# Moving the first gate's score steps into PSUM, and handing over from attention to the experts in another order

## The chip, the cores and the metric

One core of a Trainium2 chip runs the whole program. The metric is the device time of one execution in microseconds (us); lower is better. The engines are named as in the profile: PE multiplies matrices (PEld is its weight load), DVE, ACT and POOL are the vector, scalar and GpSimd engines, SP issues most transfers. [...]

## What is computed

Three layers in a row, for 2 batches of 768 tokens, 512 wide:

```
mask   = q_cluster == k_cluster            # nearest of 16 centroids per head
attn   = softmax(where(mask, q k^T / 8, -1e9)) @ v      # 8 heads of 64
x      = concat of the heads                            # 1536 x 512
noisy  = x @ w_gate + log1p(exp(x @ w_noise)) * noise   # 8 experts
top 2 of noisy, weights by softmax over the two
out    = sum over the two of  weight * relu(x @ w1[e]) @ w2[e]
y      = soft mixture (32 slots, 8 experts) of out
```

The gate (scores, top 2, the place of each token in its expert's list) is computed with small vector operations on tiles of 48 or 24 numbers a partition.

## The kernel before, in words

**Attention.** The 16 (batch, head) pairs are worked two at a time: `NP` = 8 double heads p, of 12 steps each (2 halves of the queries, `qh`, by 6 blocks of keys, `kc`). A global step number s runs from 0 to 95; the main loop of `body` takes two steps at a time (`s0`). In one turn of the loop PE gets two units of row maxima for the next double head (`munit`, tiles `pmx` and `mp`), the two steps' scores (`score`, tile `psc`), and the products with the values of the two steps before (`av`, tile `pav`). ACT takes the exponential (`pt`, five buffers). `add` sums the `pt` tiles for the denominators: POOL the first blocks (`psa`), DVE the last ones (`psb`). After each half, `ot_evac` copies the product, `den` sums the partial sums with PE (`pden`, `dt`, `rd`), and `xout` multiplies with an identity and the gate weights (`px`) and writes rows of `x` and the gate products `gp`. Tables `pre`, `mid` and `post` say at which step each such call is issued; each engine works in the order of issue.

**Gates.** `gate` returns a list of small operations and a list of scatters. Gate 0 handles chunks 0 to 5 (batch 0, finished with double head 3), gate 1 chunks 6 to 8 and gate 2 chunks 9 to 11 (the two query halves of batch 1). They stand in one list `todo`, and `gap(s, n)` issues up to n entries of it at given places of the loop; an integer in the list ends a gap. Gate 0's operations are issued from step 56 on, nearly all on DVE with operands in SBUF, at a rate from the table `RATE`; its 12 scatters (`scatter`, an indirect transfer on POOL that writes 128 rows of `x` to the lists `xg` in memory) follow with `GN` = 3 empty entries ahead of each. Gates 1 and 2 come from step 96 on and within the first steps of the expert layer.

**Expert layer (`MoE1`).** Ten lists: experts 0 and 1 of batch 0 ("short lists", jobs 0 and 1 of 256 rows), the six others for all tokens, and the short lists of batch 1. Each job has 8 steps f. A step's weights are loaded (`load_w`, four buffers `WR`), split into a high part by ACT (`split_hi`, L833) and a low part by DVE, for some steps half by POOL (`split_lo`, L840, L842), and used by `first` (L935, 12 products, then `H` by ACT and DVE) and `second` (L976, 6 products for a short list). Six splits are made in the last double head (`SP`), the others three steps ahead. `load_x` loads a list's rows on SP; `prep_t`, `prep_h`, `prep_l` transpose them on DVE and split them (L890, L897, L903). For jobs 0 and 1 the load is issued at step 80, the preparation at steps 84 to 90.

**The hand-over.** `first(0)` is issued between the scores and the last `av` of step 96. The last half's `den` and `xout` are issued in the expert layer's steps 0 and 1 (`late`), with the gate operations of batch 1 between them. `rank` of gate 1 starts with five products of the identity that nobody reads (L613).

Of the kernel before, what the change touches and what calls it, by code (L numbers as in the profile page):

```python
# [6 lines left out]
F32 = mybir.dt.float32  # L7
# [43 lines left out]
X9 = 57  # L51
DL = 64
PH, PL = 1, 1
JT, JN, JH, JL = (0, 2), 2, 2, 3
SP = 1, 3, 5, 7, 8, 9
SL, MX = 1, 96
LT = 6, 8, 9
B1 = 9
B7 = 8
B2 = 1  # L60
TF = (0, 0), (0, 1)
RATE = 2, 1, 1, 1, 2, 3, 1, 2, 1, 1, 4, 1, 3
ORD, U1, Z1, R1, Z0 = (1, 1, 1, 0, 1, 0, 1, 1), 3, 8, 4, 2
M2S = 14, 15, 16, 18, 20
MS = 10, 10, 12, 14, 18
G0, GN, KS = 55, 3, 64


class Ctx:
# [15 lines left out]
class Attention:  # L85
# [294 lines left out]
    def av(self, p, t):  # L380
        nc, g = self.nc, self.g
        qh, kc = divmod(t, 6)
        pt = self.ptile[p, t]
        if kc == 0:
            self.avp[p, qh] = g.psum.tile([128, 512], F32, tag="av", name="pav")
        for hh in range(2):
            nc.tensor.matmul(self.avp[p, qh][64 * hh:64 * hh + 64, :384], self.vt[p][:, hh, kc, :],  # L387
                             pt[:, hh, :], start=(kc == 0), stop=(kc == 5))

    def add(self, p, t):  # L390

        qh, kc = divmod(t, 6)
        pt = self.ptile
        n = 6 if p == 0 else 4 if p < MASKED else 3
        first = 0 if kc < n else n
        if kc == first:
            return
        eng = self.nc.vector if first else self.nc.gpsimd
        if kc == first + 1:
            k = "b" if first else "a"  # L400
            s = (self.g.at if first else self.g.xp).tile([128, 2, 384], F32, name=f"ps{k}", tag=f"ps{k}",
                                                         bufs=1 if first else 2)
            self.stile[p, qh, k] = s
# [15 lines left out]

    def bank(self, p, qh, name):  # L420
        g = self.g
        if p == NP - 1 and qh == 0:
            return g.psum.tile([128, 512], F32, tag="mx", name=name, bufs=2)
        return g.pm.tile([128, 512], F32, tag="misc", name=name)

    def den(self, p, qh):
        nc, g = self.nc, self.g

        parts = [self.stile.pop((p, qh, k)) for k in "ab" if (p, qh, k) in self.stile]
        terms = [(hh, s.rearrange("p h (c a j) -> p h a c j", c=3, a=4)) for s in parts for hh in range(2)]  # L430
        ps = self.bank(p, qh, "pden")
        for i, (hh, s) in enumerate(terms):
            for a in range(4):
                nc.tensor.matmul(ps[32 * a:32 * a + 32, :96], self.sel[:, hh, :], s[:, hh, a, :],
                                 start=(i == 0), stop=(i == len(terms) - 1))
# [26 lines left out]
class Dispatch:  # L462
# [67 lines left out]

    NFILL = (NSL // 128 + 1) // 2 + (NTOK + NTRASH) // 256

    def gate(self, q, first, n):

        nc, g, xp = self.nc, self.g, self.g.xp
# [5 lines left out]
        place = g.place if q == 0 else g.again  # L541

        def t(name, *shape, dt=F32):
            if name not in T and q != 1:
                m = 1
                for x in shape:
                    m *= x
                names = " ".join("abc"[:len(shape)])
                a = place(m) if dt is F32 else place(m // 2).bitcast(dt)
# [56 lines left out]
        out.append(3 if b == 0 else 1)  # L606

        def rank():
            ps = g.pm.tile([128, 512], F32, tag="misc", name="prank")
            mb = MB()  # L610

            for i in range(5 if q == 1 else 0):
                nc.tensor.matmul(ps[:, 384:], g.ident, g.ident, start=True, stop=True)  # L613
            fl = lambda a: a.rearrange("p c e -> p (c e)")
            nc.tensor.matmul(ps[:, :n * E], self.tri, fl(mb), start=True, stop=False)
            for i in range(1, n):
# [13 lines left out]
        if b == 0:  # L630
            op(dv.memset, c1[:, 0:NREG], 0.0)
# [144 lines left out]
class MoE1:  # L776
# [58 lines left out]
    def split_lo(self, s):  # L835
        nc = self.nc
        hi, lo = self.ring[s]
        wr = self.wr.pop(s)
        n = 512 if self.short[self.steps[s][0]] and not 6 <= s < 13 and s < DL else 1024
        nc.vector.tensor_tensor(lo[:, :n], wr[:, :n], f32(hi)[:, :n], op=OP.subtract)  # L840
        if n < 1024:
            nc.gpsimd.tensor_tensor(lo[:, n:], wr[:, n:], f32(hi)[:, n:], op=OP.subtract)  # L842
# [501 lines left out]
def body(tc, qk, q2, k2, v2, cent, wgn, noise, w12, phi, v12, out):  # L1344
    nc = tc.nc
    with ExitStack() as ctx:
# [93 lines left out]
        for p in range(-1, NP):  # L1440
# [24 lines left out]
            if p >= 0:  # L1465
                for qh in range(2):
                    at(post, s0 + 6 * qh + 6, A.ot_evac, p, qh)
                    for s, fn in zip(LT if p == NP - 1 else (8, 10, 12), (A.total, A.den, A.xout)):
# [28 lines left out]
        a, z = gates[1][0], [f for f in gates[2][0] if type(f) is not int]  # L1497
        i = next(i for i, f in enumerate(a) if type(f) is int and i > 10) - 13
        a, x = a[:i], [f for f in a[i:] if type(f) is not int]
        y, z = z[:21], z[21:]  # L1500
        mix(MX, a, [], 1)
        turns = y[:2] + x[:3] + y[2:6] + x[3:6]
        x, y = x[6:], y[6:]
        while x or y:
            turns += x[:1] + y[:1]
            x, y = x[1:], y[1:]
        mix(99, turns, [], 1)
        k = next(i for i, f in enumerate(z) if f.__name__ == "rank")
        mix(99, z[:k] + [1] + z[k:], gates[1][1], 3)
        mix(99, [], gates[2][1], 1)  # L1510
        half = len(todo) - half
        quota = {1: (8, 16), 2: (14, 14), 3: (14, 14)}
# [23 lines left out]
        def load_x(j):  # L1536
            assert len(todo) <= half, (len(todo), half)
            M1.load_x(j)

        for j in range(2):  # L1540
            at(post, s0 - 4, load_x, j)
            s = s0 + JT[j]
            for i in range(JN):
                at(post, s + i, M1.prep_t, j, i, JN)
                at(post, s + i + JH, M1.prep_h, j, i, JN)
                at(post, s + i + JL, M1.prep_l, j, nc.vector if i % 2 else nc.gpsimd, i, JN)
        end = 12 * NP + 2
        for s0 in range(0, end, 2):
            k = RATE[s0 // 2 - 28] if 56 <= s0 < 82 else 1 if s0 < KS else 3 if s0 < 12 * NP else 0
            units = pre.get(s0, []) + pre.get(s0 + 1, [])  # L1550
            for s in (s0, s0 + 1):
                if units:
# [5 lines left out]
            for fn, a in units + mid.get(s0, []):  # L1558
                fn(*a)
            gap(s0, k)  # L1560
            if s0 == 12 * NP:
                M1.first(0)
            for s in (s0 - 2, s0 - 1):
                if 0 <= s < 12 * NP:
                    A.av(*divmod(s, 12))
                    A.add(*divmod(s, 12))
            for s in (s0, s0 + 1):
                for fn, a in post.get(s, ()):
                    fn(*a)
                gap(s0, k)  # L1570
        late = [x for s in sorted(post) if s >= end for x in post[s]]
        c_at.close()
        c_m2 = ctx.enter_context(ExitStack())
        M1.mo = enter(c_m2, "mo2")
# [3 lines left out]
        prep = {}  # L1578
        for j in range(2):
            at(prep, 5 + j, M1.prep_m, j)  # L1580
        for j in range(2, len(M1.jobs)):
            s, n, eng = PREP[j if j in PREP else 4]
            if j > 2:
# [6 lines left out]
        for s in range(ns):  # L1590
# [10 lines left out]
            if s + 1 < ns:  # L1601
                M1.first(s + 1)
            if s < NREG * NF:
                gap(1000 if s else 98, quota.get(s, (8, 8))[0])
# [6 lines left out]
            if s < 2:  # L1611
                fn, a = late[s]
                fn(*a)
            if s < NREG * NF:
                gap(1000 if s else 98, quota.get(s, (8, 8))[1])
# [107 lines left out]
```

## Time and profile before

| | |
|---|---|
| median of 3 runs | 652.12 us (650.39 to 652.66) |
| profiled execution | 650.09 us, span 648.30 us |
| mean granted TensorE clock | 0.981 |
| PE busy | 614.9 us, 95% |
| DVE busy | 409.0 us, 63% |
| ACT busy | 311.3 us, 48% |
| POOL busy | 289.3 us, 45% |

The times of the rows below are counted from the start of the span. Attention ends at about 250 us, the expert layer at about 585 us. [...] A bracket behind a row of a timeline tells how long the engine was idle ahead of it, and which event ended that.

### The profile page before, as it was taken

The numbers are of one execution on the slowest core, as the hardware profiler recorded it, in microseconds if no ns is written. First come the engines' busy times: TensorE is split into PE (matmuls) and PEld (weight loads), VectorE is DVE, ScalarE is ACT, GpSimd is POOL, SyncE is SP. The second block draws the span as 40 slices with busy tenths as digits, with TensorE's granted clock in tenths as the row PEclk, the third lists the DMA queues.
The fourth block names the chain that finished last, engine by engine and source line by source line (L and its number), as shares of the span: only waits on it lengthen the run. The fifth ranks groups of instructions, "written<-read, shape, count | busy, mean of one in ns | idle before, by whom it ended". The sixth has DMA issues, their size and how long they took to land. (4 is left out here: it accounts for less than half of the span.)

```text
span 648.3 us, 11039 instructions
## 1 busy us (share of the span) xinstructions
PE 614.9 (95%) x3967; PEld 472.8 (73%) x3967; DVE 409.0 (63%) x871; ACT 311.3 (48%) x444; POOL 289.3 (45%) x256
## 2 busy tenths in 40 slices
PE   7899999999799999789999999999999999998996
PEld 5567666676566657667888888888888888875544
DVE  6667888778965798566554445554544557645632
ACT  5576585765556582245334334443534445533002
POOL 3899676866758793543124033251423403110100
PEclk8699999999899999989999999999999999999999
DMA  8392845727255713478944829879796868978995
GB/s 317 76 267 79 287 149 179 252 89 275 95 191 167 209 66 131 156 223 232 196 133 110 218 98 272 298 255 258 278 281 234 167 207 276 321 269 271 425 398 198
DMA packets 62890, 139.47 MB, mean 215 GB/s; under 512 B 15280, under 2 KB 30832, under 8 KB 60784
## 3 DMA queue, kind: packets, MB, share of 16 engines
q1 hardware_dynamic: 56944, 125.31, 58.3%
q0 software_dynamic: 5888, 13.42, 9.5%
q8 instruction: 32, 0.52, 0.3%
q14 instruction: 26, 0.21, 0.1%
HBM read 108.18 MB, written 28.42 MB: 211 GB/s over the span
## 5 line engine op out<-in xcount | busy, mean ns | idle before, releaser
L976 PE MATMUL py<-ring,H 128*128 128x512 f32 (+1 forms) x686 | 172.9, 396 | 5.3 <-issue 3.5
L840 DVE TENSOR_TENSOR ring<-wr,ring 128x1024 fp32r<-128x1024 f32 (+1 forms) x77 | 93.5, 1214 | 100.4 <-ACT ring L833 99.5
L976 PEld LDWEIGHTS py<-ring,H 128*128 128x128 f32 (+1 forms) x686 | 123.9, 184 | 32.5 <-issue 3.8
L833 ACT ACTIVATE ring<-wr 128x1024 fp32r<-128x1024 f32 x77 | 81.5, 1059 | 91.7 <-PE py L976 83.6
L377 ACT ACTIVATE pt<-psc 128x768 f32<-128x768 f32 x96 | 77.2, 811 | 71.1 <-PE psc L374 60.8
L984 POOL DMA_INDIRECT x2acc<-y,mdi x31 | 50.2, 1621 | 104.4 <-ACT y L1009 97.6
L387 PE MATMUL pav<-pt,vt 128*64 128x384 f32 x384 | 73.6, 505 | 0.0
L941 ACT ACTIVATE H<-ph 128x256 fp32r<-128x256 f32 (+7 forms) x80 | 36.7, 459 | 75.9 <-PE ph L935 60.9
L338 DVE TENSOR_REDUCE mp<-pmx 128x1 f32<-128x512 f32 x96 | 63.2, 676 | 15.3 <-PE pmx L333 14.4
L935 PE MATMUL ph<-XS1a,ring 128*128 128x240 f32 (+3 forms) x288 | 67.8, 325 | 0.0
L407 POOL TENSOR_TENSOR psa<-psa,pt 128x768 f32<-128x768 f32 x32 | 61.9, 1936 | 4.7 <-ACT pt L377 2.5
L935 PE MATMUL ph<-XS0a,ring 128*128 128x432 f32 (+3 forms) x252 | 63.2, 332 | 0.1
L944 DVE SCALAR_TENSOR_TENSOR H<-ph,H 128x384 fp32r<-128x384 f32 (+2 forms) x120 | 43.4, 389 | 26.3 <-ACT H L941 20.6
L935 PEld LDWEIGHTS ph<-XS1a,ring 128*128 128x128 f32 x288 | 47.7, 188 | 3.6 <-DVE ring L840 0.2
L935 PE MATMUL ph<-XS0b,ring 128*128 128x256 f32 (+3 forms) x192 | 48.2, 325 | 0.8 <-DVE ring L840 0.6
L935 PE MATMUL ph<-XS1b,ring 128*128 128x240 f32 (+3 forms) x192 | 46.1, 313 | 0.8 <-DVE ring L840 0.8
L935 PEld LDWEIGHTS ph<-XS0a,ring 128*128 128x128 f32 x252 | 43.2, 188 | 4.0 <-issue 1.2
L903 POOL TENSOR_TENSOR XS0b<-xr,XS0a 128x512 fp32r<-128x512 f32 (+1 forms) x9 | 17.1, 1901 | 64.5 <-ACT XS0a L897 64.5
L387 PEld LDWEIGHTS pav<-pt,vt 128*64 128x64 f32 x384 | 23.5, 137 | 24.8 <-issue 19.3
L333 PE MATMUL pmx<-even 96*128 96x512 f32 (+1 forms) x96 | 34.0, 415 | 6.2 <-DVE mp L338 4.3
L343 DVE TENSOR_REDUCE mp<-pmx 128x2 f32<-128x512 f32 x48 | 33.0, 689 | 5.5 <-PE pmx L333 5.0
L638 POOL DMA_INDIRECT xg<-x,idx x24 | 25.9, 1077 | 21.1 <-DVE xr L567 14.8
(338 smaller groups left out, 1023.7 us busy)
## 6 DMA issues: line engine op xcount, KB each, us to landing
wr<-in_w SPq DMA_DIRECT2D x80, 512.0 KB
v<-in_v SPq DMA_DIRECT2D x9, 2048.0 KB
xg<-xr SPq DMA_DIRECT2D x14, 512.0 KB
wr<-in_qk SPq DMA_DIRECT2D x8, 768.0 KB
early<-in_q SPq DMA_DIRECT2D x8, 768.0 KB
early<-in_k SPq DMA_DIRECT2D x8, 768.0 KB
x2acc<-xr SPq DMA_DIRECT2D x8, 512.0 KB
vt<-in_v SPq DMA_DIRECT2D x8, 384.0 KB
```

Source lines behind the costliest of these rows:

```text
L333: nc.tensor.matmul(o, self.BQ[i][:96, qh, hh, 128 * c:128 * c + 128], self.BK[i][:96, hh, ks], start=True, stop=True)
L338: nc.vector.tensor_reduce(mp[:, 0, col:col + 1], ps, axis=AX.X, op=OP.max)
L377: nc.scalar.activation(pt, ps[:, :, :384], AF.Exp, scale=SCALE)
L387: nc.tensor.matmul(self.avp[p, qh][64 * hh:64 * hh + 64, :384], self.vt[p][:, hh, kc, :], pt[:, hh, :], start=(kc == 0), stop=(kc == 5))
L407: eng.tensor_tensor(s, s, pt.pop((p, t)), op=OP.add)
L833: self.nc.scalar.activation(self.ring[s][0], self.wr[s], AF.Copy)
L840: nc.vector.tensor_tensor(lo[:, :n], wr[:, :n], f32(hi)[:, :n], op=OP.subtract)
L935: nc.tensor.matmul(ph[:, :u], a[:, 128 * c:128 * c + 128], x[:, c, :u], start=(c == 0 and i == 0), stop=(c == 3 and i == 2))
L941: nc.scalar.activation(HH[:, :u], ph[:, :u], AF.Relu)
L944: nc.vector.scalar_tensor_tensor(o[:, :b - a], ph[:, a:b], 0.0, f32(HH)[:, a:b], op0=OP.max, op1=OP.subtract)
L976: nc.tensor.matmul(o, x, y, start=(f == 0 and i == 0), stop=(f == NF - 1 and i == 2))
L984: st = nc.gpsimd.indirect_dma_start(out=out, out_offset=bass.IndirectOffsetOnAxis(ap=di, axis=0), in_=y, in_offset=None, compute_op=OP.add)
```

## The change

- **Gate 0** gets a function of its own. Its two score tiles PL and PW lie in the unused last 128 columns of the bank that `av` writes (`g.spare`); the bank is now one tile for the whole of attention. Operations with such an operand carry the mark `ps`, and are issued only right behind the two `av` calls of a turn, up to four at a time. Other small operations go from DVE to POOL. `gap` issues one entry at a time.
- **Scatters of gate 0**: two right behind the gate, the other ten at steps 78, 81, 84, 84, 85, 85, 86, 86, 87, 88 (`SC`).
- **Short lists**: both loads at step 90; job 0 is prepared at steps 96 and 97, all on ACT and DVE; job 1 in steps 2 and 3 of the expert layer.
- **Hand-over**: the last `pt` tile isn't added to `psb` but summed by `den` itself; `den` and `xout` of the last half are issued at step 96. Gate 1's first five operations are issued at step 95, eleven at step 96 behind the last `av`; twelve, and one of gate 2, behind the preparation of job 0; then `first(0)`. The five identity products are gone.
- **Splits**: four instead of six ahead of the expert layer, so `split` 4 and 5 and the loads 8 and 9 come in its first steps; before step 13 DVE makes the whole low part.

```
-JT, JN, JH, JL = (0, 2), 2, 2, 3
-SP = 1, 3, 5, 7, 8, 9
-SL, MX = 1, 96
-LT = 6, 8, 9
+JX, JT, JN = 6, (12, 2), 2
+SC = -6, -3, 0, 0, 1, 1, 2, 2, 3, 4
+LEAD = 5, 16
+SP = 1, 3, 5, 7
+SL, MX = 1, 94
+LT = (6, 8, 9), (6, 6, 6)
...
 def av(self, p, t):
+        if (p, t) == (0, 0):
+            bank = g.psum.tile([128, 512], F32, tag="av", name="pav")
+            self.avb, g.spare = bank[:, :384], bank[:, 384:]
         if kc == 0:
-            self.avp[p, qh] = g.psum.tile([128, 512], F32, tag="av", name="pav")
+            self.avp[p, qh] = self.avb
 def add(self, p, t):
-        if kc == first:
+        if kc == first or (p, t) == (NP - 1, 11):
             return
 def den(self, p, qh):
+        if (p, 6 * qh + 5) in self.ptile:
+            parts.append(self.ptile.pop((p, 6 * qh + 5)))
+    def gate0(self, n):
...
+        PL, PW = (lambda i=i: g.spare[:, 8 * n * i:8 * n * i + 8 * n].rearrange("p (c e) -> p c e", e=E) for i in range(2))
+        def op(f, *a, **k):
...
+            run.ps = any(x is PL or x is PW for x in a)
+            out.append(run)
+        TTn, TR, STT = dv.tensor_tensor, dv.tensor_reduce, dv.scalar_tensor_tensor
+        PT, PS = gp.tensor_tensor, gp.tensor_scalar
+        top = lambda o, x: op(TR, o, x, axis=AX.X, op=OP.max)
+        op(TR, U, gl(1), axis=AX.X, op=OP.add)
+        op(TR, PL, gl(0), axis=AX.X, op=OP.add)
...
+        op(PT, N, N, self.noise[:, :n], op=OP.mult)
+        out.append(3)
+        op(TTn, PL, N, PL, op=OP.add)
+        top(M0, PL)
+        op(TTn, PW, PL, lambda: bcn(M0()), op=OP.is_equal)
+        op(TTn, PW, PW, bce(self.iode), op=OP.mult)
+        top(V0, PW)
+        op(TTn, oh[0], PW, lambda: bcn(V0()), op=OP.is_equal)
+        op(STT, PL, oh[0], -1e30, PL, op0=OP.mult, op1=OP.add)
+        op(PS, wcol(0), V0, -1.0, float(E), op0=OP.mult, op1=OP.add)
...
 def rank():
-            for i in range(5 if q == 1 else 0):
-                nc.tensor.matmul(ps[:, 384:], g.ident, g.ident, start=True, stop=True)
 def split_lo(self, s):
-        n = 512 if self.short[self.steps[s][0]] and not 6 <= s < 13 and s < DL else 1024
+        n = 512 if self.short[self.steps[s][0]] and 13 <= s < DL else 1024
 body:
-        for f in gates[0][1]:
-            todo += [(G0, None)] * GN + [(G0, f)]
+        todo += [(G0, f) for f in gates[0][1][:2]]
...
+        mix(MX, a[:LEAD[0]], [], 1)
+        mix(96, a[LEAD[0]:LEAD[1]], [], 1)
...
-        def gap(s, n):
-            while n > 0 and todo and todo[0][0] <= s:
+        def gap(s, n, bank=False):
+            while n > 0 and todo and todo[0][0] <= s and (bank or not getattr(todo[0][1], "ps", False)):
...
+        for f, s in zip(gates[0][1][2:], SC):
+            at(post, s0 + s, f)
         for j in range(2):
-            at(post, s0 - 4, load_x, j)
+            at(post, s0 + JX, load_x, j)
...
-            k = RATE[s0 // 2 - 28] if 56 <= s0 < 82 else 1 if s0 < KS else 3 if s0 < 12 * NP else 0
+            k = 1 if s0 < MX else 0
...
-            if s0 == 12 * NP:
-                M1.first(0)
             for s in (s0 - 2, s0 - 1):
                 if 0 <= s < 12 * NP:
                     A.av(*divmod(s, 12))
+            gap(s0, 4 * k, True)
+            for s in (s0 - 2, s0 - 1):
+                if 0 <= s < 12 * NP:
                     A.add(*divmod(s, 12))
+            if s0 == 12 * NP:
+                gap(s0, 30)
...
+        gap(1000, lead[0])
+        M1.first(0)
+        gap(1000, lead[1])
```

## Rows read from the trace of the kernel before

**Rows 1.** Windows: six-step stretches, then the last double head, hand-over, burst of scatters.
```profile
core 0: us, PE busy (x) PEld busy (x) DVE busy (x) ACT busy (x) POOL busy (x), PEclk, DMA share, GB/s
146.16:160.47 14.31, 14.07 (x108) 9.23 (x107) 11.86 (x23) 8.64 (x15) 9.97 (x6) 1.00 0.86 298
160.47:179.41 18.94, 15.12 (x101) 9.92 (x100) 17.45 (x41) 9.74 (x14) 11.56 (x6) 0.91 0.32 98
179.41:193.32 13.91, 13.46 (x107) 9.28 (x105) 10.06 (x29) 8.24 (x12) 8.07 (x6) 1.00 0.50 185
193.32:206.35 13.03, 13.03 (x101) 9.16 (x99) 8.46 (x18) 8.93 (x12) 11.76 (x9) 1.00 0.41 138
206.35:221.62 15.27, 13.39 (x101) 9.11 (x99) 9.24 (x19) 7.51 (x11) 14.01 (x10) 1.00 0.79 262
221.62:246.81 25.19, 24.05 (x216) 16.18 (x214) 23.47 (x34) 18.18 (x25) 21.64 (x12) 1.00 0.34 84
246.81:273.94 27.13, 25.29 (x198) 21.46 (x196) 20.61 (x88) 6.24 (x17) 10.18 (x10) 1.00 0.42 138
273.94:281.96 8.02, 4.56 (x20) 3.85 (x20) 2.39 (x7) 2.02 (x4) 5.38 (x6) 0.80 0.79 275
```

**Rows 2.** Timeline in the first gate: start, duration, engine, what, idle before.
```profile
169.80 1.63 DVE L567 SCALAR_TENSOR_TENSOR xr<-ohe,xr 128x48 f32<-128x48 f32 x1
...
171.96 1.33 DVE L567 TENSOR_SCALAR x<-xr 128x6 f32<-128x6 f32 x1
172.09 0.51 PE L333 MATMUL pmx<-even 96*128 96x256 f32 x2 [3.33 <-DVE mp L338]
```

**Rows 3.** Windows right behind the two long PE pauses (columns as rows 1).
```profile
172.09:176.30 4.21, 4.21 (x14) 2.19 (x15) 3.41 (x7) 0.70 (x2) 4.13 (x3) 0.59 0.51 179
...
277.40:281.28 3.88, 3.88 (x16) 3.17 (x17) 2.11 (x6) 0.90 (x2) 2.83 (x3) 0.66 0.59 206
```

**Rows 4.** Lines of DVE with a PSUM operand: count, ns least/median/most, first and last start.
```profile
L454 DVE TENSOR_TENSOR x<-px,rd x32: 310/348/358, 58.1 to 258.0; 128x192 f32<-128x192 f32 x32
L620 DVE TENSOR_TENSOR xr<-prank,ebase x2: 184/191/198, 182.3 to 266.8; 128x48 f32<-128x48 f32 x1, 128x24 f32<-128x24 f32 x1
```

**Rows 5.** Timeline behind four scatters in a row in attention.
```profile
207.87 0.97 POOL L638 DMA_INDIRECT xg<-x,idx  x1 [0.30 <-issue]
...
209.85 0.28 DVE L437 STREAM_TRANSPOSE dt<-pden 128x96 f32<-128x96 f32 x1 [4.14 <-PE psc L374]
```

**Rows 6.** Timeline: pieces of the hand-over, and gate 1's rank.
```profile
237.53 1.08 PE L451 MATMUL px<-iw,ot 128*128 128x160 f32 x6
240.03 2.40 DVE L407 TENSOR_TENSOR psb<-psb,pt 128x768 f32<-128x768 f32 x1
253.24 0.51 PE L434 MATMUL pden<-psb,sel 128*32 128x96 f32 x16
253.82 0.28 DVE L437 STREAM_TRANSPOSE dt<-pden 128x96 f32<-128x96 f32 x1 [0.19 <-PE pden L434]
258.83 1.28 PE L613 MATMUL prank<-ident 128*128 128x128 f32 x10
261.89 0.17 PE L615 MATMUL prank<-mb,tri 128*128 128x24 bf16 x1 [1.78 <-DVE mb L567]
```

**Rows 7.** Lines of the lists' preparation (columns as rows 4).
```profile
L890 DVE STREAM_TRANSPOSE xr<-xr x4: 664/684/698, 229.5 to 233.3; 128x512 f32<-128x512 f32 x4
L897 ACT ACTIVATE XS0a<-xr x2: 613/622/631, 230.2 to 231.7; 128x512 fp32r<-128x512 f32 x2
L903 DVE TENSOR_TENSOR XS1a<-xr,XS1a x2: 685/685/685, 527.8 to 532.0; 128x512 fp32r<-128x512 f32 x2
```

**Rows 8.** Timeline in the burst of scatters of gates 1 and 2.
```profile
276.96 0.38 ACT L941 ACTIVATE H<-ph 128x256 fp32r<-128x256 f32 x1 [5.85 <-remote]
...
277.40 1.89 PE L976 MATMUL py<-ring,H 128*128 128x512 f32 x6 [3.46 <-issue]
```

**Rows 9.** SP's queue: the first short list's load.
```profile
218.36 1.89 SPq L856 DMA_DIRECT2D xr<-xg  x4
```

More of the change, by code (lines that the diff above doesn't have):

```diff
@@ L61 @@
 TF = (0, 0), (0, 1)
-RATE = 2, 1, 1, 1, 2, 3, 1, 2, 1, 1, 4, 1, 3
 ORD, U1, Z1, R1, Z0 = (1, 1, 1, 0, 1, 0, 1, 1), 3, 8, 4, 2
@@ L65 @@
 MS = 10, 10, 12, 14, 18
-G0, GN, KS = 55, 3, 64
+G0 = 55
 class Ctx:
@@ L421, in bank @@
         g = self.g
-        if p == NP - 1 and qh == 0:
+        if p == NP - 1 and (qh == 0 or name == "pden"):
             return g.psum.tile([128, 512], F32, tag="mx", name=name, bufs=2)
@@ L533, in gate @@
     def gate(self, q, first, n):
+        if q == 0:
+            return self.gate0(n)
         nc, g, xp = self.nc, self.g, self.g.xp
@@ L540, in gate @@
         T = {}
-        place = g.place if q == 0 else g.again
         def t(name, *shape, dt=F32):
@@ L548, in t @@
                 names = " ".join("abc"[:len(shape)])
-                a = place(m) if dt is F32 else place(m // 2).bitcast(dt)
+                a = g.again(m) if dt is F32 else g.again(m // 2).bitcast(dt)
                 T[name] = a.rearrange(f"p ({names}) -> p {names}", **dict(zip("abc", shape)))
@@ L605, in gate @@
         op(TTn, wcol(2), TT, wcol(1), op=OP.mult)
-        out.append(3 if b == 0 else 1)
+        out.append(1)
         def rank():
@@ L629, in gate @@
         op(TR, Q, W2, axis=AX.X, op=OP.add)
-        if b == 0:
-            op(dv.memset, c1[:, 0:NREG], 0.0)
         op(dv.tensor_copy, self.idx[:, :, cs], Q)
@@ L1467, in body @@
                     at(post, s0 + 6 * qh + 6, A.ot_evac, p, qh)
-                    for s, fn in zip(LT if p == NP - 1 else (8, 10, 12), (A.total, A.den, A.xout)):
+                    for s, fn in zip(LT[qh] if p == NP - 1 else (8, 10, 12), (A.total, A.den, A.xout)):
                         at(post, s0 + 6 * qh + s, fn, p, qh)
@@ L1492, in body @@
         mix(G0, gates[0][0], [], 1)
-        for f in gates[0][1]:
-            todo += [(G0, None)] * GN + [(G0, f)]
+        todo += [(G0, f) for f in gates[0][1][:2]]
         half = len(todo)
[L1497 to L1504, printed above, removed]
+        a, z = [f for f in gates[1][0] if type(f) is not int], [f for f in gates[2][0] if type(f) is not int]
+        at_rank = lambda x: next(i for i, f in enumerate(x) if f.__name__ == "rank")
+        n1, n2 = at_rank(a), at_rank(z)
+        mix(MX, a[:LEAD[0]], [], 1)
+        mix(96, a[LEAD[0]:LEAD[1]], [], 1)
+        x, y = a[n1 + 1:], z[9:n2]
+        turns = a[LEAD[1]:n1] + z[:9] + a[n1:n1 + 1]
+        while x:
             turns += x[:1] + y[:1]
@@ L1507, in body @@
         mix(99, turns, [], 1)
-        k = next(i for i, f in enumerate(z) if f.__name__ == "rank")
-        mix(99, z[:k] + [1] + z[k:], gates[1][1], 3)
+        mix(99, y, gates[1][1], 2)
+        mix(99, z[n2:], [], 1)
         mix(99, [], gates[2][1], 1)
         half = len(todo) - half
-        quota = {1: (8, 16), 2: (14, 14), 3: (14, 14)}
-        def gap(s, n):
-            while n > 0 and todo and todo[0][0] <= s:
+        quota = {0: (19, 9), 1: (9, 0), 2: (14, 14), 3: (14, 14)}
+        lead = n1 - LEAD[1] + 1, 4
+        def gap(s, n, bank=False):
+            while n > 0 and todo and todo[0][0] <= s and (bank or not getattr(todo[0][1], "ps", False)):
                 t, fn = todo.pop(0)
@@ L1538, in load_x @@
             M1.load_x(j)
+        for f, s in zip(gates[0][1][2:], SC):
+            at(post, s0 + s, f)
         for j in range(2):
-            at(post, s0 - 4, load_x, j)
[L1542 to L1546, printed above, removed]
+            at(post, s0 + JX, load_x, j)
+        for i in range(JN):
+            at(post, s0 + JT[0], M1.prep_t, 0, i, JN)
+            at(post, s0 + JT[0] + 1, M1.prep_h, 0, i, JN)
+            at(post, s0 + JT[0] + 1, M1.prep_l, 0, nc.vector, i, JN)
         end = 12 * NP + 2
         for s0 in range(0, end, 2):
-            k = RATE[s0 // 2 - 28] if 56 <= s0 < 82 else 1 if s0 < KS else 3 if s0 < 12 * NP else 0
+            k = 1 if s0 < MX else 0
             units = pre.get(s0, []) + pre.get(s0 + 1, [])
@@ L1569, in body @@
                     fn(*a)
-                gap(s0, k)
-        late = [x for s in sorted(post) if s >= end for x in post[s]]
+                gap(s0, 30 if s == MX + 1 else k)
+        assert max(post) < end
+        gap(1000, lead[0])
+        M1.first(0)
+        gap(1000, lead[1])
         c_at.close()
@@ L1580, in body @@
             at(prep, 5 + j, M1.prep_m, j)
+        for i in range(JN):
+            at(prep, JT[1] + i, M1.prep_t, 1, i, JN)
+            at(prep, JT[1] + i + 1, M1.prep_h, 1, i, JN)
+            at(prep, JT[1] + i + 1, M1.prep_l, 1, nc.vector, i, JN)
         for j in range(2, len(M1.jobs)):
@@ L1603, in body @@
             if s < NREG * NF:
-                gap(1000 if s else 98, quota.get(s, (8, 8))[0])
+                gap(1000, quota.get(s, (8, 8))[0])
             if s == ns - 1:
@@ L1610, in body @@
                 M1.second(s)
-            if s < 2:
-                fn, a = late[s]
-                fn(*a)
             if s < NREG * NF:
-                gap(1000 if s else 98, quota.get(s, (8, 8))[1])
+                gap(1000, quota.get(s, (8, 8))[1])
             if s == OV:
```

77 lines of the change are left out of this document (added).

## Prediction

> **What bounds the kernel now.** I read the windows first. In six undisturbed steps PE is busy for the whole stretch: 13.03 of 13.03 us, 14.07 of 14.31 [rows 1]. So PE sets the pace, and an edit is worth what it does to PE's pauses and clock, not to busy sums. Three stretches around the change are out of step. The first holds the first gate: 18.94 us, where its neighbours take 14.31 and 13.91. The second ends with four scatters in a row: 15.27 us, 1.88 of them without PE work. The third lies in the burst of twelve scatters: 8.02 us, with 4.56 of PE work at a clock of 0.80.
>
> The timeline then says why, for the first. DVE executes in order, and the maxima that free PE's bank stand behind gate operations of 1.63 and 1.33 us on tiles of 48 and 6 numbers; PE waited 3.33 us for them [rows 2]. An operation of the same width with an operand in PSUM took 0.18 to 0.20 us [rows 4]. [...]
>
> Profiled, the program took 650.09 us (span 648.30), 2.03 less than the median of 652.12. I make the sum on the profiled execution and lay it on the median.
>
> **The change part by part.**
>
> *First gate.* I followed the list through the new `gap`: scores' sums at turn 56, the exponential part to turn 60, the fourteen top-2 operations on the spare columns in turns 62, 64, 66 and 68, rank at 72, the last index copy and two scatters at 74. Of some fifty operations DVE keeps about twenty, and those of the top 2 read one operand in PSUM. The two that held PE become about 0.2 us each, or go to POOL, where nothing of PE waits behind them at once. What goes is 18.94 - (14.31 + 13.91) / 2 = 4.83 us. A larger gain is excluded, since the neighbours are PE-bound. What is added: `av` and these DVE operations now share a bank, so DVE must wait for the products of its turn and the next products for DVE. Rows of before have no such wait. From below it costs nothing: DVE idles through the products today, and the next turn's products come a turn (13.03 / 3 = 4.3 us) later. From above, each of four turns pays all its operations, 4 x 4 x 0.2 = 3.2 us. I take 0.6, since DVE is busy for 8 to 12 of 14 us in the neighbours [rows 1]. Net **-4.2** (-4.8 to -1.6).
>
> [...]
>
> *Scatters.* Four in a row start again at step 84, and `psa` stands behind them on POOL. At 0.97 us and 0.3 between [rows 5] that is 5.1 us; `psa` of the first two blocks came when its buffers were not yet wanted, five buffers deep, so no new wait by the count. In before DVE's transposition started 4.14 us late behind such four [rows 5], and PE lost 1.88 us. I don't know the cause; the weight loads that ran beside them stay at step 74, where now only two scatters are. I take half, **-0.9** (-1.9 to +1). The last double head has 25.19 - 24.05 = 1.14 us of PE pauses with preparation and splits around them; these leave it for the most part: **-0.4** (-1.1 to +1).
>
> *Hand-over.* What goes: the wait of 1.78 for rank and 1.28 for the identity products [rows 6], 3.1 us. What comes: `first(0)` was PE's work between the last products; now nothing stands behind them but sums and x, while job 0's rows are prepared only after x. Count from the end of the last `av`. PE: 24 sums (16 take 0.51, so 0.8) and `px` 1.08 [rows 6], done at 1.9; the copy by ACT lies beside the sums. DVE: `psb` beside a POOL addition takes 2.4 [rows 6] and ends about with `av`; then eleven gate operations of 0.2, 2.3 with gaps; then three operations on the denominators, 0.7; x and gates, two of 0.35 and a third [rows 4], 0.9; two transpositions 1.4; high part on ACT 0.62; low parts 0.69 each, of which one lies beside the second high part [rows 7]. If DVE is up to date at `px`: 1.9 + 0.9 + 1.4 + 1.3 = 5.5, and PE pauses 3.5. If the gate operations are still in front: 2.3 + 0.7 + 0.9 + 1.4 + 1.3 = 6.6 to 6.8, a pause of 4.9. I take 4.2, and 1.5 for the clock behind it [rows 3]. DVE then owes some 45 gate operations of 0.2 (9 us) and job 1's 2.8 [rows 7] beside its part of each step, so an H may come late: 0.4 (0 to 1). 4.2 + 1.5 + 0.4 - 3.1 = **+3.0** (+1.7 to +4.5).
>
> The list's load is moved too. Its two times five transfers pass SP at step 90, behind a weight load and the landing of the last scatter. In before they were issued from 218.36 [rows 9], and the first transposition ran at 229.5 [rows 7]: landing takes at most 11 us. From turn 90 to that transposition there are three turns and 3 us, about 15. That covers it, with some 4 us to spare; SP's next weight load, behind it, is wanted only five steps into the expert layer.
>
> *Burst.* Twelve scatters still follow each other on POOL, at nearly the same time. In before ACT's H started 5.85 us late there and PE waited 3.46 [rows 8]; with the clock, 3.46 + 0.20 x 8.02 = 5.1 us. I leave it: **0** (-5.1 to +5.1). Two splits more in the expert layer are hidden by PE's steps as the later ones are; without that cover each would be a DVE operation of about 1.2 us.
>
> Sum: -4.2 - 0.9 - 0.4 + 3.0 + 0 = **-2.5 us**: 647.6 for an execution such as the profiled one, 649.6 on the median.
>
> **The rivals.**
>
> *The bursts lose their stall.* If it needs scatters, weight loads and a late DVE together, the new order may break it up: -2.5 - 1.0 - 5.1 = -8.6, 643.5 us. For it: the stall came only in two places, both with runs of scatters beside weight loads. Against: both are still there in the expert layer.
>
> *The shared bank makes PE wait.* The full 3.2 is paid, -2.5 + 2.6 = +0.1, 652.2 us. For it: DVE is the busiest engine after PE in these turns. Against: it idles during products now.
>
> *Slower: weight loads meet the scatters.* Loads 8 and 9, which went out ahead of the expert layer, are now issued when splits 4 and 5 free their buffers, that is with the scatters, as 10 and 11 are already. If the stall grows with the loads beside it, from two to four, it doubles: -2.5 + 5.1 = +2.6, 654.7 us. It decides as soon as load 8, issued in step 3, hasn't landed when split 8 is issued in step 5, since split 8 then holds ACT and every H behind it. For it: that is where ACT waited for something that the profile calls remote [rows 8]. Against: the loads are a fifth to a third of the bytes there (my estimate from 0.26 MB a scatter and 0.5 MB a load: 1.0 of 5.2 MB).
>
> *The change doesn't do what it says*: the spare-bank operations are stretched as those of before, and the first 4.2 stay lost: +1.7, 653.8 us. Against: 32 operations with a PSUM operand lie between 310 and 358 ns, whatever POOL did [rows 4].
>
> **How the numbers follow.** 0.3% of the median is 2.0 us, about what a measurement of this kernel tells from no change. Forecast 0.42 (its own range 647.6 to 651.6), bursts freed 0.24, bank 0.16, loads 0.15, no effect 0.03. Faster: two thirds of the forecast and the freed bursts, 0.52. Same: the rest of the forecast and most of the bank, 0.27. Slower: 0.21. The range goes from the freed bursts to the loads, 643 to 655.
>
> **What would show it.** Right: six steps across the gate in 14 to 15 us, at a clock of 1.00; gate operations of DVE near 0.2 us; a PE pause of 3.5 to 5 us between the last `px` and the first product of the expert layer, ended by DVE's low part, with a lower clock behind it; no identity products. Wrong: `pav` waiting for a gate operation by more than 0.5 us in a turn; a pause at `first(0)` ended by a transfer, or under 2 us or over 7; first products of steps 7 and 8 waiting for a split; or the burst's pause gone, which would make the forecast too slow by five.

## Result, and the profile after

The changed kernel took 645.93 us (median of 11 runs, 641.11 to 647.84), the kernel before 651.13 beside it (11 runs, 649.25 to 652.66): ratio 0.990, 95% interval 0.9875 to 0.9924; the medians lie 5.2 us apart (their quotient is 0.992). The times of the changed kernel lie in two groups, five from 641.11 to 643.47 and six from 645.93 to 647.84. The profiled execution is of the lower group and took 643.45 us (span 641.7, mean granted clock 0.981), 6.6 us less in span than the one before. The granted clock is a share of full speed; its records hold 1.00 and 0.50 alone, in this trace and in that of the kernel before.

These are the windows of the changed kernel between the same events as [rows 1] (first sum of the denominators, `pden`, of each half; the last two rows run to `pden` of the second half of the last double head, and on to the first product of step 8 of the expert layer). Columns as there.

```profile
145.69:159.51 13.82, 13.82 (x108) 9.32 (x106) 10.90 (x23) 8.74 (x15) 10.64 (x9) 1.00 0.88 307
159.51:172.60 13.09, 13.09 (x101) 9.22 (x99) 10.01 (x24) 9.41 (x13) 5.05 (x6) 1.00 0.23 70
172.60:186.93 14.33, 13.17 (x100) 9.18 (x98) 10.74 (x26) 8.33 (x13) 12.93 (x11) 1.00 0.61 206
186.93:200.15 13.22, 13.22 (x107) 9.39 (x106) 8.80 (x22) 7.46 (x10) 10.83 (x16) 1.00 0.21 53
200.15:215.55 15.40, 13.43 (x100) 9.07 (x98) 11.58 (x19) 8.98 (x12) 14.84 (x9) 1.00 0.53 203
215.55:241.97 26.42, 25.41 (x224) 16.72 (x222) 20.70 (x34) 14.55 (x21) 17.96 (x13) 1.00 0.46 153
241.97:271.93 29.96, 25.79 (x204) 22.89 (x202) 25.11 (x96) 11.53 (x24) 12.10 (x11) 0.94 0.63 182
```

The second row is the gate: 13.09 us, all of it PE work at full clock, where before had 18.94 [rows 1]; DVE is busy for 10.01 us in it instead of 17.45. The scatters' stretch has not become shorter (15.40 after 15.27).

The gate's operations on the spare columns, DVE's rows in the timeline of the changed kernel, as the counterpart of [rows 2] (`pav` lies in PSUM, as every tile that PE writes in these kernels, `xr` in SBUF); the last row is PE's only pause over 0.03 us from 145 to 202 us:

```profile
169.00 0.21 DVE L572 TENSOR_TENSOR pav<-xr,pav 128x48 f32<-128x48 f32 x1 [0.86 <-PE pav L391]
172.72 0.21 DVE L572 TENSOR_REDUCE xr<-pav 128x6 f32<-128x48 f32 x1 [0.76 <-PE pav L391]
177.29 0.21 DVE L572 TENSOR_REDUCE xr<-pav 128x6 f32<-128x48 f32 x1 [0.76 <-PE pav L391]
183.35 0.21 DVE L572 TENSOR_REDUCE xr<-pav 128x6 f32<-128x48 f32 x1 [0.83 <-PE pav L391]
181.29 0.50 PE L334 MATMUL pmx<-even 96*128 96x256 f32 x2 [1.16 <-DVE mp L339]
```

Each turn DVE waits 0.76 to 0.86 us for the products before its first operation on the shared bank. The trace shows no wait of PE's `pav` for a gate operation. PE's one pause is for row maxima (`mp`).

The hand-over in the changed kernel, the counterpart of [rows 6]: timeline, then the window behind the pause.

```profile
243.28 1.08 PE L457 MATMUL px<-iw,ot 128*128 128x160 f32 x6
244.67 0.28 DVE L443 STREAM_TRANSPOSE dt<-pden 128x96 f32<-128x96 f32 x1
246.17 1.29 DVE L1001 STREAM_TRANSPOSE xr<-xr 128x512 f32<-128x512 f32 x2
248.18 0.39 PE L1046 MATMUL ph<-XS0a,ring 128*128 128x256 f32 x1 [3.82 <-ACT XS0a L1008]
253.27 0.19 PE L728 MATMUL prank<-mb,tri 128*128 128x24 bf16 x1
```

```profile
248.18:252.50 4.32, 3.97 (x19) 3.77 (x20) 3.32 (x16) 0.87 (x4) 0.00 (x0) 0.63 0.00 2
```

PE pauses 3.82 us ahead of the expert layer, the clock behind it is 0.63, and rank no longer waits.

### The profile page after: what moved, and what is told of

It reads as the page before. It is cut to its first block, busy times and chain, and to the rows that moved or that the text cites. A ratio compares the mean times of both kernels' runs of the same rounds, so it can differ in the third digit from the quotient of the medians.

```text
span 641.7 us, 11046 instructions
## 1 busy us (share of the span) xinstructions
PE 612.6 (95%) x3973; PEld 472.6 (74%) x3973; DVE 404.5 (63%) x856; ACT 311.1 (48%) x444; POOL 282.5 (44%) x268
## 5 line engine op out<-in xcount | busy, mean ns | idle before, releaser
L391 PE MATMUL pav<-pt,vt 128*64 128x384 f32 x384 | 72.3, 498 | 0.0
L1046 PE MATMUL ph<-XS0a,ring 128*128 128x432 f32 (+3 forms) x252 | 64.6, 340 | 4.3 <-ACT XS0a L1008 3.8
L1046 PEld LDWEIGHTS ph<-XS0a,ring 128*128 128x128 f32 x252 | 44.8, 197 | 7.4 <-ACT XS0a L1008 4.1
L1046 PE MATMUL ph<-XS0b,ring 128*128 128x256 f32 (+3 forms) x192 | 46.6, 316 | 2.1 <-ACT ring L944 1.5
L749 POOL DMA_INDIRECT xg<-x,idx x24 | 28.0, 1168 | 26.8 <-DVE inv L682 20.0
```

Of the source, the lines that this page charges most:

```text
L1046: nc.tensor.matmul(ph[:, :u], a[:, 128 * c:128 * c + 128], x[:, c, :u], start=(c == 0 and i == 0), stop=(c == 3 and i == 2))
```

## A second pair of traces, and PE's late signals

With the experiments below, the kernel before was timed again on three chips, called A, B and C, and the changed kernel on B and C. Only on B was each of the two traced. A was used for the gate alone, the tiles in SBUF, the operations of gate 1 behind the list and the first run without the burst. All runs of a chip were made together, so chip and time of the runs aren't told apart.

*The changed kernel and the kernel before, once more.* No edit.

> The changed kernel once more, beside the variants, on the chip of this call. Theory A (of its 5.2 us, some 2.5 to 3 come from the steps of the prediction, the rest from PE's late signals among scatters, which the first pair of traces has and the four traces of the first experiments have not): where no signal is late, 642 to 644 us against 645 to 647 of the kernel before, ratio 0.994 to 0.997. Theory B (the whole gain belongs to the change): ratio 0.988 to 0.992 here too.

> The kernel before once more, for its trace. Theory A: where it takes 645 to 647 us instead of 651, no end of a product is told to the other engines over 0.3 us late, the burst of twelve scatters has no pause over 1 us, and the six steps across the gate still take 18 to 19 us. Theory B: the burst's pause of 3.5 us is there again, and the lower time comes from another stretch.

On chip B the changed kernel took 641.88 us against 646.56 (12 and 29 runs), ratio 0.9945 (0.9927 to 0.9964): theory A's range, and theory B's lies outside the interval. The trace of the kernel before, too, has what its theory A asks: no late signal, no pause over 1 us in the burst, and 18.91 us across the gate. The two pairs side by side, by the same events, in us:

| stretch | before | after | change | before, B | after, B | change |
|---|---|---|---|---|---|---|
| up to six steps ahead of the gate | 146.16 | 145.69 | -0.47 | 146.23 | 145.62 | -0.61 |
| six steps ahead of the gate | 14.31 | 13.82 | -0.49 | 14.34 | 13.82 | -0.52 |
| across the gate | 18.94 | 13.09 | -5.85 | 18.91 | 13.09 | -5.82 |
| next two stretches | 26.94 | 27.55 | +0.61 | 26.92 | 27.55 | +0.63 |
| scatters in a row | 15.27 | 15.40 | +0.13 | 15.26 | 15.40 | +0.14 |
| to `pden` of the last double head's first half | 19.77 | 20.47 | +0.70 | 19.78 | 19.16 | -0.62 |
| hand-over and steps 0 to 7 | 37.79 | 35.91 | -1.88 | 33.74 | 37.11 | +3.37 |
| steps 8 to 15 | 29.63 | 28.86 | -0.77 | 28.89 | 27.78 | -1.11 |
| rest of the span | 339.5 | 340.9 | +1.4 | 339.5 | 340.2 | +0.6 |
| span | 648.3 | 641.7 | -6.6 | 643.6 | 639.7 | -3.9 |

From six steps ahead of the gate to the scatters the stretches repeat within 0.03 us. The kernel before differs mainly in one place: hand-over and burst, 37.79 against 33.74, and that is the whole difference of its spans but 0.65. The changed kernel differs in two: 20.47 against 19.16 up to `pden` of the last double head's first half, and 35.91 against 37.11 behind it. The pause of [rows 8] is not there on chip B. The same place in the timeline of the kernel before, chip B: ACT makes the H of that step, with the scatters around it as dense as before.

```profile
269.24 0.97 POOL L638 DMA_INDIRECT xg<-x,idx  x1 [0.31 <-issue]
270.52 1.29 POOL L638 DMA_INDIRECT xg<-x,idx  x1 [0.30 <-issue]
271.19 0.38 ACT L941 ACTIVATE H<-ph 128x256 fp32r<-128x256 f32 x1 [1.54 <-PE ph L935]
272.12 0.97 POOL L638 DMA_INDIRECT xg<-x,idx  x1 [0.30 <-DVE H L944]
273.95 0.39 ACT L941 ACTIVATE H<-ph 128x256 fp32r<-128x256 f32 x1 [1.43 <-PE ph L935]
```

What `remote` in [rows 8] stood for can be worked out from the trace, which also holds the times of semaphore updates, the signals by which an engine tells the others that an instruction is done. I paired PE's updates, in order, with the PE instructions that make one (some 650 a trace) and took the time from an instruction's end to its update: 0.014 us at the median. The largest, and those over 0.5 us:

```
trace                          largest  over 0.5 us, and where
before                         7.31     11: 208.3-210.0 (scatters in a row), 269.8-281.4 (burst)
after                          1.16      6: 217.5-221.8 (scatters in a row), 274.7 (end of burst)
chips A and B, eight traces    0.07      0
chip C: changed kernel         1.25      9: 217.8-222.3, 260.7, 275.3
chip C: operations behind      3.88      7: 221.8-222.0, 233.7, 278.8
chip C: same, tiles in SBUF    3.47      6: 221.3-222.2, 278.0
chip C: list first, second try 1.36      7: 217.7-222.1
```

DVE's and ACT's updates, paired alike, are never over 0.03 us late, and their parts of H take 0.42 and 0.39 us in the burst with late signals and without; whether a recorded end of theirs can hold a delay at all, the trace doesn't tell. So in the first pair and on chip C, and only while scatters run on POOL (once beside a single one, at 233.7), the other engines learn late of PE's products, counted from the modelled ends; on chips A and B they don't in any of eight traces, six of them with all the scatters. The `dt` of [rows 5] stood behind such an update (2.61 us late), and ACT's H of [rows 8] behind another (5.80); they started 0.03 and 0.08 us behind these updates, so the delay is no matter of the pairing. The rows of the timeline don't show it by themselves, since the profile models the ends of products. Whether PE's work or only the signal is late, and whether the scatters cause it, no run here shows.

*The changed kernel a third time, chip C.* No edit.

> The changed kernel a third time, as the measure for the three variants beside it: ratio 0.993 to 0.996 to the kernel before where PE's signals are on time (0.9945 the second time), 0.988 to 0.992 where they are late.

It took 642.59 us against 654.95 (6 and 11 runs), ratio 0.9836 (0.979 to 0.9882), below what I expected for either case. Its trace has late signals; the kernel before is 8.4 us slower than on chip B, the changed one 0.7. That the kernel before loses so much to late signals is argued only, as it wasn't traced on chip C. So one kernel pair has ratios from 0.984 to 0.995 by the chip and time of its runs.

## The experiments on the parts

**The gate alone**, in the kernel before:

```
+ gate0, its bank and gap(..., bank) as in the changed kernel
-RATE = 2, 1, 1, 1, 2, 3, 1, 2, 1, 1, 4, 1, 3
+RATE = 1, 1, 1, 1, 1, 1, 1, 1, 1, 2, 4, 3, 3
```

> The kernel before with the first gate's part alone: score tiles in the spare columns of the products' bank, operations on them issued right behind the products, the other small ones on POOL; scatters, lists, hand-over and splits stay as before. Theory (first gate worth 4.2 to 6 us, nothing else needed for it): six steps across the gate in 13 to 14.5 us instead of 18.94, 646 to 647 us where the kernel before takes 651, ratio 0.990 to 0.9935. Rival (the stretch is only short because scatters and splits are moved too): over 15 us for the six steps, ratio above 0.996. The stall among the last twelve scatters stays in either case.

649.82 us (7 runs) against 646.25 on chip A: ratio 1.0059 (1.0039 to 1.008), 0.6% slower. Yet across the gate it has 13.11 us. What it gains there it loses behind: from 200.25 to 255.11, 54.86 us, where the kernel before on chip B takes 46.53. Windows and ACT's timeline in that stretch:

```profile
208.00:212.00 4.00, 3.71 (x12) 3.06 (x12) 3.86 (x9) 2.40 (x4) 3.22 (x4) 0.56 0.49 191
218.94:224.00 5.06, 2.24 (x40) 1.68 (x38) 1.89 (x5) 0.00 (x0) 4.38 (x4) 1.00 0.41 157
```

```profile
206.36 0.81 ACT L377 ACTIVATE pt<-psc 128x768 f32<-128x768 f32 x1 [3.20 <-POOL psa L410]
224.20 1.51 ACT L377 ACTIVATE pt<-psc 128x768 f32<-128x768 f32 x2 [6.96 <-POOL psa L407]
```

Neither theory: the gate's steps are short without the other parts, but twelve scatters issued within four turns keep POOL from `psa`, the buffers of `pt` run out, and ACT and then PE wait (PE 3.88 us, up to 225.06), with a clock of 0.56 behind the first of these waits. My edit packs the scatters tighter than before: POOL runs them from 199.4 to 222.3 us, in the kernel before from 187.0 to 215.4. How much of the loss the old spacing would bring stays open; what follows is that with scatters as close as these the gate's gain is more than lost.

**The first gate's tiles in SBUF**, in the changed kernel, and on chip C with the operations of gate 1 behind (next paragraph):

```
-PL, PW = (... g.spare[:, 8 * n * i:8 * n * i + 8 * n] ...)
+PL, PW = (lambda k=k: t(k, n, E) for k in ("pl", "pw"))
```

> The changed kernel with the first gate's two score tiles in SBUF; places of issue and the move of small operations to POOL stay. Theory A (PSUM makes the operations short): DVE's operations on them lengthen beside POOL's additions as in before (over 0.5 us in places, 1.3 to 1.6 at worst), PE waits for row maxima again in these steps, 2 to 5 us more than the changed kernel, ratio 0.993 to 0.998. Theory B (the place behind the products and POOL's share are enough): operations near 0.2 to 0.4 us, no wait of PE, same ratio as the changed kernel, 0.990.

643.30 us (8 runs), ratio 0.9963 (0.9935 to 0.9992). This ratio alone fits theory A, and its interval overlaps that of the changed kernel on chip B; the trace decides. Across the gate 13.09 us, as with the bank; the four stretches from 145.80 to 199.80 take 54.00 us where the changed kernel on chip B takes 54.46. DVE's rows, with POOL's and PE's:

```profile
172.20 0.21 DVE L572 TENSOR_TENSOR ohe<-xr 128x48 f32<-128x48 f32 x1
176.27 1.84 POOL L306 TENSOR_TENSOR even<-early,even 64x768 fp32r<-64x768 f32 x1
176.77 1.42 DVE L572 TENSOR_TENSOR xr<-xr 128x48 f32<-128x48 f32 x1
180.94 0.50 PE L334 MATMUL pmx<-even 96*128 96x256 f32 x2 [0.71 <-DVE mp L339]
182.31 0.52 DVE L572 TENSOR_TENSOR ohe<-xr 128x48 f32<-128x48 f32 x1
```

Theory B. Two operations still lengthen beside a POOL operation: the first takes 1.42 us, until 0.08 us behind its end (178.11), the second 0.52 us, until 0.06 us behind another's (182.77). But right behind the products nothing that PE waits for stands at once behind them. The bank avoids the long operations (0.21 to 0.22 us each for the top 2 on it, first trace of the changed kernel) and pays with DVE's waits (0.76 to 0.86 us a turn); the two come out 0.46 us apart, which is PE's one pause, 1.16 us with the bank and 0.71 without. On chip C the pair with the operations of gate 1 behind, 643.42 with the bank and 644.29 without, is the same within the 1 us expected there if the bank is worth nothing by itself.

**Gate 1's eleven operations behind the list's preparation**, in the changed kernel: `LEAD = 5, 16` becomes `5, 5`.

> The changed kernel with the eleven operations of gate 1 that stand ahead of the last denominators moved behind the preparation of the first short list. Theory A (these operations set the pause at the first product of the expert layer): the pause falls from 3.82 us to 1.5 to 2.5, 1.5 to 3 us faster than the changed kernel, ratio 0.985 to 0.988. Theory B (they must be paid anyway): the pause falls but rank or a late H takes its place, same time as the changed kernel within 1 us.

> The changed kernel with the eleven operations of gate 1 behind the preparation of the list, once more beside the changed kernel on one chip. Theory A (they set a part of the pause, 1.1 us of its 3.8): pause at the first product 2.7 to 2.8 us, 1 to 2 us faster than the changed kernel in this call. Theory B (given back by rank or a late H): same within 0.5 us.

> The same with the first gate's score tiles in SBUF. If the bank is worth nothing by itself (with tiles in SBUF the six steps across the gate took 13.09 us as with the bank, and its operations 0.19 to 0.21 us), the time is that of the variant without it, within 1 us; if operations beside POOL's additions lengthen again in front of row maxima, 1 us or more slower.

Chip A: 640.39 us (6 runs), ratio 0.9915 (0.9898 to 0.9932). Chip C: 643.42, ratio 0.984 (0.9792 to 0.9889), and with tiles in SBUF 644.29, ratio 0.9836 (0.979 to 0.9881), beside the changed kernel's 0.9836. First product of the expert layer, chips A and C:

```profile
246.77 0.39 PE L1046 MATMUL ph<-XS0a,ring 128*128 128x256 f32 x1 [2.75 <-ACT XS0a L1008]
```

```profile
251.32 0.39 PE L1046 MATMUL ph<-XS0a,ring 128*128 128x256 f32 x1 [2.75 <-ACT XS0a L1008]
```

The pause falls to 2.75 us: less than the first theory A had (1.5 to 2.5), and as the second, which was written after that trace, has it. But on one chip with the changed kernel no gain is left to see (643.42 against 642.59): there that kernel's own pause was 3.22, and late signals took more from the variant than from it, just ahead (PE paused 3.15 us, in the changed kernel 0.37). Timeline of the variant on chip C:

```profile
217.47 0.97 POOL L749 DMA_INDIRECT xg<-x,idx  x1 [0.30 <-issue]
221.85 0.28 DVE L443 STREAM_TRANSPOSE dt<-pden 128x96 f32<-128x96 f32 x1 [5.41 <-remote]
223.17 0.50 PE L334 MATMUL pmx<-oddb 96*128 96x256 f32 x2 [3.15 <-DVE mp L339]
```

Whether the order is worth a microsecond stays open; on chip A the changed kernel itself wasn't timed.

**The list prepared ahead of the last denominators**, in the changed kernel:

```
-JX, JT, JN = 6, (12, 2), 2
+JX, JT, JN = 5, (12, 2), 2
-LEAD = 5, 16
+LEAD = 5, 5
-quota = {0: (19, 9), 1: (9, 0), 2: (14, 14), 3: (14, 14)}
-lead = n1 - LEAD[1] + 1, 4
+quota = {0: (6, 6), 1: (6, 4), 2: (4, 6), 3: (12, 12)}    # second try {0: (8, 8), 1: (4, 0), 2: (3, 6), 3: (10, 12)}
+lead = 2, 4                                               # second try 4, 8
+post[s0 + JT[0]] = rows + post.get(s0 + JT[0], [])        # rows: prep_t, prep_h, prep_l of job 0
```

The second try also gives half of `split_lo` of steps 4 to 6 to POOL.

> The changed kernel with another hand-over: the first short list is loaded a step earlier, ahead of a weight load that waits, and prepared ahead of the last denominators; the gate operations of the second batch all come behind the first product of the expert layer, six at a time, and rank of gate 1 behind the third second product. Theory A (the pause of 3.8 us is only the order of DVE's work): pause under 1 us, no lower clock behind it, 4 to 5 us faster than the changed kernel, ratio to it 0.993. Theory B (the work is only put off): rank, an H or the scatters come late, PE waits 2 us or more within the first five steps, and the gain is under 2 us.

> The list prepared ahead of the last denominators, as in the first try, but with eight gate operations at a time, rank of gate 1 a half step earlier, rank of gate 2 a step later than in the changed kernel, and half of the low part of steps 4 to 6 on POOL. Theory A (the first try lost its gain to DVE's queue: rank 1.75 us late, low parts 0.75 and 0.95, weights 2.9): these waits shrink below 1 us in sum up to 290 us, and the time falls 2 to 4 us below the changed kernel. Theory B (DVE has the same work before the scatters in any order, and the weights come late in any case): no faster than the changed kernel.

First try, chip B: 643.89 us (12 runs), ratio 0.9971 (0.9952 to 0.999). Second, chip C: 643.85 (6 runs), 0.9861 (0.9817 to 0.9905). Neither is faster than the changed kernel on its chip (641.88 and 642.59), and theory B holds. The pause is gone, and from `pden` of the last double head's first half to the first product it is 8.74 us in both, against 12.55 (changed kernel, chip B). But steps 8 to 15 take 30.34 and 32.02 us instead of 27.78. Timeline of the first try:

```profile
263.82 0.19 PE L728 MATMUL prank<-xr,tri 128*128 128x24 bf16 x1 [1.75 <-DVE xr L682]
296.32 3.23 PE L1046 MATMUL ph<-XS0b,ring 128*128 128x256 f32 x12 [2.88 <-ACT ring L944]
```

and of the second:

```profile
294.63 1.06 ACT L944 ACTIVATE ring<-wr 128x1024 fp32r<-128x1024 f32 x1 [6.82 <-DMA wr<-in_w]
295.74 3.23 PE L1046 MATMUL ph<-XS0b,ring 128*128 128x256 f32 x12 [4.14 <-ACT ring L944]
```

In the second the first eight steps keep the gain (24.63 us, the changed kernel 24.56), and PE then stands where the weights have not landed; the twelve products behind it take 3.23 us, at a clock of 0.50, where others take 1.6. From the same `pden`, that product starts after 58.86 and 58.67 us in the two tries, and after 58.57 in the changed kernel on chip B, where PE waits 0.41 us for its weights: what comes ahead of it has been shortened by 3.8 us, and it is no earlier. Part of the hand-over's pause is therefore cover for transfers, as far as these three traces show: without it a wait appears 50 us later.

**Without the burst**: the changed kernel with the twelve scatters dropped from the list, then with empty entries in their places.

```
-mix(99, y, gates[1][1], 2)
+mix(99, y, [], 2)              # second: [None] * len(gates[1][1])
-mix(99, [], gates[2][1], 1)
+                               # second: mix(99, [], [None] * len(gates[2][1]), 1)
```

> The changed kernel without the twelve scatters of gates 1 and 2 (left out: the rows of the second batch are not put into the lists). The times of the changed kernel lie in two groups, 641 to 643.5 and 646 to 648 us. Theory A (the upper group is the one in which PE's signals come late among these scatters, as in the profile of before): one group is left, all executions within 639 to 643.5 us, and no product's end is told late in the expert layer. Theory B (the groups come from elsewhere, such as the loads of weights or the end of the program): two groups 5 us apart remain.

> The changed kernel without the twelve scatters of gates 1 and 2 (left out: the second batch's rows are not put into the lists), with empty entries in their places, so that the operations around them keep theirs. Theory A (the burst costs PE nothing where no signal is late): same time as the changed kernel in this call within 1 us. Theory B (transfers of the burst hold up weights or lists later): 2 us or more faster, with the pause near 292 us gone.

The first, chip A: 644.97 us (12 runs, 642.97 to 646.33), ratio 0.9979 (0.9966 to 0.9993): neither theory, one group, but higher than A has it. An entry of the list also paces what stands behind it; without the scatters gate 2's rank is issued a step early and PE waits for it:

```profile
257.20 0.19 PE L728 MATMUL prank<-xr,tri 128*128 128x24 bf16 x1 [2.03 <-DVE xr L682]
```

The second, chip B: 641.82 us, the changed kernel 641.88 beside it. Where signals are on time, twelve scatters cost PE nothing that shows. The two groups of times that I meant to explain stay open: on chip B all twelve runs of the changed kernel lie in the lower one (640.27 to 643.33), on chip C four do and two lie in the upper one (645.90 and 646.92), so the chip alone doesn't make them.

No variant was shown to beat the changed kernel.

## Why the prediction was right, point by point

The range of 643 to 655 us holds the 645.93. The forecast's own range, 647.6 to 651.6, doesn't: the 5.2 us at the medians are twice the 2.5 forecast. What the terms are worth is best read on chip B, where no signal is late.

*First gate, -4.2: right in kind, too small.* The four stretches around it give -0.5, -5.8 and +0.6, so -5.7 on both pairs. The term mis-sized is the base: I took the neighbours' mean of 14.11 for what the six steps could fall to and called a larger gain excluded; they fell to 13.09, and the stretch ahead, which holds the gate's first operations, lost 0.5 as well. The six steps lie below the 14 to 15 us that I named as a sign. My 0.6 for the shared bank is about what the comparison with SBUF gives (0.46). What PSUM itself was to bring was wrong: the tiles in SBUF do the same, so the gain is the place of issue and the operations that POOL took; no run tells these two apart.

*Scatters, -0.9: wrong,* +0.14. PE's 1.9 to 2.0 us of pauses there are in all four traces. On chip B, first before, then after, the longest is ended by row maxima that stand on DVE behind `psb`, lengthened beside POOL operations (`psb<-pt` takes 0.95 us at the median, 14 of them in the first trace of the kernel before):

```profile
210.23 3.09 DVE L404 TENSOR_TENSOR psb<-pt 128x768 f32<-128x768 f32 x1
216.03 0.50 PE L333 MATMUL pmx<-oddb 96*128 96x256 f32 x2 [1.54 <-DVE mp L338]
```

```profile
203.97 1.75 DVE L408 TENSOR_TENSOR psb<-pt 128x768 f32<-128x768 f32 x1
205.82 2.41 DVE L411 TENSOR_TENSOR psb<-psb,pt 128x768 f32<-128x768 f32 x1
209.87 0.50 PE L334 MATMUL pmx<-oddb 96*128 96x256 f32 x2 [1.79 <-DVE mp L339]
```

In the changed kernel the run of scatters starts only behind this pause (210.05), so it needs none. In the first trace of the kernel before, PE's 1.88 us came behind DVE's late `dt` instead (the 4.14 us of [rows 5] are idle time, 2.61 of them the lateness of the update), and I halved a pause that didn't go away with the order. What the spacing alone is worth, no run shows.

*Last double head -0.4 and hand-over +3.0: right, in part by luck.* -0.62 and +3.37 on chip B, +2.75 together against 2.6. The pause was to be 4.2 and is 3.82 and 3.83; the clock behind it 1.5, between the 4.21 x 0.41 = 1.7 and 3.88 x 0.34 = 1.3 of [rows 3], and is 4.32 x 0.37 = 1.6 in the first pair, but 4.81 x 0.50 + 6.00 x 0.10 = 3.0 on chip B:

```profile
247.19 0.58 PE L1046 MATMUL ph<-XS0a,ring 128*128 128x256 f32 x1 [3.83 <-ACT XS0a L1008]
```

```profile
247.19:252.00 4.81, 4.65 (x20) 4.36 (x21) 3.32 (x16) 1.02 (x5) 0.00 (x0) 0.50 0.01 4
252.00:258.00 6.00, 6.00 (x39) 5.38 (x39) 3.77 (x27) 1.33 (x5) 1.13 (x2) 0.90 0.00 0
```

The clock's term was thus half of what chip B shows, and the shorter pause and the late H that didn't come (0.4 each) make up for about half of that. Rank's wait and the identity products are gone. The list's rows had landed: `prep_t` follows `gp` without a wait for a transfer. The pause ends with the list's high part on ACT, not with DVE's low part as the prediction's sign says; the low part holds PE for another 0.35 us (chip B 0.16).

*Burst, 0 with 5.1 to either side: not a price of the change.* The stall comes with the late signals. In the first pair they cost the kernel before some 4 us there (37.79 against 33.74); the changed kernel took 1.3 us more than on chip B in the stretch ahead, where its own late signals lie, and 1.2 less in this one, with the higher clock behind its pause. That makes most of the difference between -6.6 and -3.9 in span. My 5.1 counted the clock over the pause as well; with [rows 3] it would be 3.46 + 1.3 = 4.8. One sign of being wrong came true: the burst's pause is gone from the changed kernel's first trace (no pause of PE over 0.2 us from 249 to 278 us), which was to make the forecast too slow. The rival "bursts lose their stall" thus describes the first pair of traces, but not its reason: on chip B both kernels are without the stall.

*The other rivals.* The bank never made `pav` wait for a gate operation; loads 8 and 9 among the scatters held nothing up (on chip B PE is busy for all of 254.30 to 273.00); the spare-bank operations were as short as forecast (0.21 to 0.22 us).

*Not foreseen:* steps 8 to 15, -0.8 and -1.1. On chip B a split waits less for its weights (PE's pause 1.42 us before, 0.41 after). In the first pair it is the other way round, 1.50 us after and none over 0.4 there before; there the kernel before starts step 8 at the low clock behind the burst's pause (0.66, [rows 3]).

With signals on time the sum was -2.5 and is -3.9 in span. The gate's 1.5 is as much as the difference, but only since the other misses cancel: +1.0 for the scatters and +0.4 for the hand-over against -1.1 in steps 8 to 15 and -0.2 in the last double head.

## What to carry to other kernels

Small vector operations cost what stands behind them on their engine (PE's 3.33 us in [rows 2]): issue them where nothing is queued that the busy engine needs, and look at the memory of their operands only then (13.09 us across the gate with either memory). Before a stall is priced from one trace, take a second one on another chip: of 6.6 us in span here 3.9 were left there. A pause in front of a stretch that is fed by transfers may be their cover, so ask what arrives late once it is gone (here weights, 2.88 and 4.14 us).

## What the runs showed of the hardware that was not expected

- Other engines can learn of PE's finished products up to 7.31 us late behind the modelled end while scatters run on POOL, in all six traces of the first pair and chip C and in none of the eight of chips A and B (0.07 us at most). What differs, the chip or something else at the time, no run shows. The traces with late updates also miss records of updates (739 for DVE's 753 operations in the first trace of the changed kernel, 735 for 752 on chip C; 755 on chip B), those without at most one of an engine's.
- After the same pause of 3.8 us the same program got a clock of 0.63 for 4.3 us in one execution, and of 0.50 and then 0.90 for 10.8 us in another: 1.4 us between two executions of one kernel.
